# Double-width GpSimd products, e in place of d, fourth buffers and a new order in a fused recurrence and highway layer

## Chip, cores and metric

The kernel runs on one core of a Trainium2 chip. The metric is device time in microseconds (us) of one execution, the median of several runs. Engines are named as the profile has them: PE is TensorE, DVE is VectorE, ACT is ScalarE, POOL is GpSimd, SP is the engine that issues the DMAs.

## The reference

Four sequences of 6,336 tokens with 256 channels pass a gated recurrence and then a highway layer:

```python
sig = 1.0 / (1.0 + np.exp(-f_logit))
f = lower_bound + (1.0 - lower_bound) * sig
for t in range(S):
    h = f[:, t] * h + (1.0 - f[:, t]) * x[:, t]
    y[:, t] = h
...
H = np.maximum(y @ w_h, 0.0)
T = 1.0 / (1.0 + np.exp(-(y @ w_t + b_t)))
return T * H + (1.0 - T) * y
```

Inputs and output are float32. `lower_bound` and `b_t` have 256 entries, the weights are 256 x 256.

## The kernel before

The 25,344 tokens are cut into 28 units (L42 to L71): two of 256 tokens, one of 512, twenty-three of 1,024, one of 512, one of 256. Every unit passes the same operations, each a small function `do_<letter>`. The text `order` (L72 to L124) is a list of such operations, and it alone sets the program: `f12.1:2` calls `do_f` for unit 12, half 1, with buffer 2, a `v` behind it puts the operation on VectorE, and a number behind the colon is the buffer. Operations are kept in this order on each engine (`keep_in_program_order`); between engines only data and buffers hold them. All loads and writes stand in SP's one queue, so a write that waits for its copy holds up the loads behind it.

For one unit of 1,024 tokens, with channels in two halves of 128:

- l and x (L260): loads of 1 MB each, tokens on the partitions, in 6 buffers each.
- u (L274): ScalarE, sigmoid of -l, 3 buffers.
- bv (L282): u times x, in pairs of token blocks (512 columns an instruction, four instructions), on GpSimd or VectorE, 3 buffers.
- uT and bT (L288, L308): TensorE transposes u and bv so that channels lie on the partitions and tokens along the columns. f (L299, or L297 on VectorE) is made of uT.
- y (L325): VectorE's scan along the tokens, the recurrence, from f and bT. It carries its last value from unit to unit, and a unit that holds the start of a sequence has two scans for a half.
- z and g (L337 and L140): TensorE's products of y with the two weights, for each half. t (L350): ScalarE's sigmoid of z. d (L354): VectorE, from y and g, 3 buffers.
- e = d times t (L359), in a tile of its own, 3 buffers. The last field of a unit is a cut: columns below it go to GpSimd in pieces of 512 (`do_E`), the rest in one VectorE instruction (`do_e`).
- op (L378, L379): TensorE transposes back and adds, y through `diag` and e through the identity. o (L388): the copy to SBUF, mostly on ScalarE. Then the write (L393) of 512 KB.

`shared` (L203) makes a GpSimd product wait for the VectorE product (or weight preparation) that stands last ahead of it in the order text:

```python
def shared(ins, gpsimd):
    if not gpsimd:
        held[:] = [ins]
    elif held:
        tc.add_manual_dep(ins.ins, held.pop().ins.name, ...)
```

Ahead of the units stand the parameters (`cc`, `dg`, `WH`, `WT`) and idle matmuls that keep TensorE's clock up (`k*16`, L149 to L153).

## Time and profile before

| what | value |
|---|---|
| three executions | 211.55, 211.85 and 212.19 us, median 211.85 |
| profiled execution: span | 210.1 us (the page gives no other time of it; the median is 1.75 us more) |
| busy: PE, DVE, ACT, POOL | 192.2, 193.0, 194.5 and 174.0 us |
| DMA | 78.69 MB, on average 374 GB/s |
| instructions | 4,667 |

A group of instructions in the profile is shown as line, engine, operation, output <- inputs with shape and type, x its number | busy us, mean ns of one | the engine's idle time just before them and what ended it. In the timeline the columns are start, length, engine, line and operation, and in brackets the idle time before and what ended it. Neighbouring VectorE instructions overlap by some 0.09 us in their records and GpSimd's by some 0.05, so what one costs its engine is the distance of two starts.

### The profile page before, as it was taken

What the parts mean: (1) busy time and instruction counts of PE and PEld (TensorE: products, weight loads), DVE (VectorE), ACT (ScalarE), POOL (GpSimd) and SP (SyncE); (2) the same over time, 40 slices, a digit from 0 to 9 for tenths busy, and PEclk for the clock granted to TensorE, in tenths of its full rate; (3) what the DMA queues carried; (4) which work ended last, traced back from release to release, by engine and by line L of the source; (5) the groups of instructions that cost most, each with busy time, mean ns of one, the idle gap of its engine ahead of it and who ended that gap; (6) DMA issues with size and microseconds to landing.
All of it is one profiled execution on the core that took longest, in us unless ns stands there. A gap on an engine that the chain in (4) does not pass through costs nothing.

```text
span 210.1 us, 4667 instructions
## 1 busy us (share of the span) xinstructions
PE 192.2 (91%) x1819; PEld 132.4 (63%) x1819; DVE 193.0 (92%) x154; ACT 194.5 (93%) x190; POOL 174.0 (83%) x166
## 2 busy tenths in 40 slices
PE   7967798899989989999999999999999899999981
PEld 2444555576655766767576667657775676776760
DVE  0689999999999999999999999999999999999950
ACT  4678999999999999999999999999999999997882
POOL 3068989789999599978999999889879969999630
PEclk9999999999999999999999999999999999999998
DMA  6999999999999999999999999999999998463486
GB/s 223 392 426 421 410 418 424 420 415 420 410 428 413 420 420 403 331 406 387 387 427 416 409 416 423 418 417 396 333 428 416 416 413 332 188 271 132 172 328 254
DMA packets 15982, 78.69 MB, mean 374 GB/s; under 512 B 1748, under 2 KB 2264, under 8 KB 10072
## 3 DMA queue, kind: packets, MB, share of 16 engines
q1 hardware_dynamic: 15952, 78.39, 92.9%
q8 instruction: 14, 0.23, 0.5%
q14 instruction: 8, 0.07, 0.1%
q10 hardware_dynamic: 8, 0.00, 0.0%
HBM read 52.43 MB, written 25.95 MB: 373 GB/s over the span
## 4 chain that ended last, share of the span: by engine, by line
DVE 34%; PE 34%; DMA 12%; issue 8%; POOL 5%; ACT 3%; SPq 1%; POOLq 0%; DVEq 0%; ACTq 0%
DVE y L325 21%; DMA x<-in_x_dram 12%; DVE d L354 10%; PE op L379 5%; PE op L378 5%; PE g L337 4%; PE z L337 4%; PE bT L308 4%; POOL bv L282 4%; PE g L140 4%; PE uT L288 4%; PE z L140 3%; DVE e L359 3%; ACT t L350 2%; ACT o L388 1%
## 5 line engine op out<-in xcount | busy, mean ns | idle before, releaser
L282 POOL TENSOR_TENSOR bv<-u,x 128x512 bf16<-128x512 f16 x96 | 110.2, 1178 | 22.3 <-DVE w_sb L235 8.9
L325 DVE TENSOR_TENSOR_SCAN y<-f,y,bT 128x1024 bf16<-128x1024 f16 (+5 forms) x54 | 107.2, 1994 | 1.4 <-issue 0.4
L359 POOL TENSOR_TENSOR e<-d,t 128x512 bf16<-128x512 bf16 (+1 forms) x59 | 65.0, 1125 | 8.3 <-DVE e L359 5.0
L354 DVE SCALAR_TENSOR_TENSOR d<-y,ncc,g 128x1024 bf16<-128x1024 bf16 (+2 forms) x56 | 63.1, 1140 | 1.8 <-PE g L337 1.3
L350 ACT ACTIVATE t<-z,bt 128x1024 bf16<-128x1024 f32 (+2 forms) x56 | 58.4, 1066 | 2.7 <-PE z L140 1.5
L299 ACT ACTIVATE f<-uT,ncc 128x1024 f16<-128x1024 f16 (+2 forms) x54 | 57.8, 1079 | 2.0 <-ACT f L299 1.0
L388 ACT COPY o<-op 128x1024 f32<-128x1024 f32 (+1 forms) x50 | 52.3, 1058 | 1.9 <-PE op L379 1.0
L274 ACT ACTIVATE u<-l 128x2048 f16<-128x2048 f32 (+2 forms) x28 | 49.0, 1760 | 4.1 <-DMA l<-in_f_logit_dram 4.1
L378 PE MATMUL op<-diag,y 128*128 128x128 f16 x396 | 49.4, 219 | 0.8 <-ACT t L350 0.5
L379 PE MATMUL op<-ident_b,e 128*128 128x128 bf16 x396 | 49.4, 219 | 0.6 <-POOL e L359 0.6
L379 PEld LDWEIGHTS <-e 128*128 128x128 bf16 x396 | 44.0, 113 | 4.6 <-POOL e L359 1.1
L378 PEld LDWEIGHTS <-y 128*128 128x128 bf16 x396 | 44.2, 113 | 2.5
L337 PE MATMUL z<-y,w_sb 128*128 128x512 bf16 (+1 forms) x112 | 39.2, 367 | 2.0 <-DVE d L354 1.0
L337 PE MATMUL g<-y,w_sb 128*128 128x512 bf16 (+1 forms) x112 | 39.6, 367 | 0.5 <-DVE y L325 0.3
L308 PE MATMUL bT<-ident_f,bv 128*128 128x128 f32 x198 | 31.9, 278 | 4.1 <-DVE y L325 1.9
L288 PE MATMUL uT<-ident_h,u 128*128 128x128 f16 x396 | 31.1, 220 | 4.5 <-DVE y L325 3.3
L288 PEld LDWEIGHTS <-u 128*128 128x128 f16 x396 | 26.3, 98 | 13.9 <-issue 7.4
L140 PE MATMUL g<-y,w_sb 128*128 128x512 bf16 x92 | 34.9, 379 | 0.0
L140 PE MATMUL z<-y,w_sb 128*128 128x512 bf16 x92 | 34.8, 379 | 0.0
L337 PEld LDWEIGHTS <-w_sb 128*128 128x128 f16 x224 | 21.6, 98 | 16.2 <-issue 0.8
L308 PEld LDWEIGHTS bT<-ident_f,bv 128*128 128x128 f32 x198 | 22.3, 141 | 12.0 <-POOL bv L282 4.5
L140 PEld LDWEIGHTS <-w_sb 128*128 128x128 f16 x184 | 17.9, 98 | 18.2 <-issue 3.9
(35 smaller groups left out, 47.1 us busy)
## 6 DMA issues: line engine op xcount, KB each, us to landing
out_dram<-o SPq DMA_DIRECT2D x48, 512.0 KB, 6.1
l<-in_f_logit_dram SPq DMA_DIRECT2D x23, 1024.0 KB, 10.2
x<-in_x_dram SPq DMA_DIRECT2D x23, 1024.0 KB, 11.1
l<-in_f_logit_dram SPq DMA_DIRECT2D x2, 512.0 KB, 9.2
x<-in_x_dram SPq DMA_DIRECT2D x2, 512.0 KB, 6.0
l<-in_f_logit_dram SPq DMA_DIRECT2D x3, 256.0 KB, 6.1
x<-in_x_dram SPq DMA_DIRECT2D x3, 256.0 KB, 5.4
out_dram<-o SPq DMA_DIRECT2D x3, 256.0 KB, 5.4
```

The source lines that it names most:

```text
L140: return pe.add_instruction(mybir.InstMatmult(name=nc.get_next_instruction_name(), start_tensor_calc=start, stop_tensor_calc=stop, tile_si ...
L282: shared(pin(e.tensor_mul(st[n]["bv"][:, k].rearrange("p d j -> p j d"), st[n]["u"][:, q:q + 2], st[n]["x"][:, q:q + 2])), not eng)
L288: pin(nc.tensor.transpose(uT[:, j * P:(j + 1) * P], st[n]["u"][:, j, h * P:(h + 1) * P], ident_h))
L299: pin(nc.scalar.activation(to, of, AF.Identity, scale=ncc[:, h:h + 1], bias=1.0))
L308: pin(nc.tensor.transpose(words[:, k:k + g * (P - 1) + 1:g], pair, ident_f))
L325: pin(nc.vector.tensor_tensor_scan(y[:, c:e], st[n]["f", h][:, c:e], st[n]["bT", h][:, c:e], 0.0 if fresh else carry[h], op0=ALU.mult, op1 ...
L337: pin(nc.tensor.matmul(p[:, a:e], w, half(n, "y", ki)[:, a:e], start=ki == 0, stop=ki == NH - 1))
L350: pin(nc.scalar.activation(half(n, "t", m), st[n]["z", m][:, :tokens(n)], AF.Sigmoid, bias=bt[:, m:m + 1]))
L354: pin(nc.vector.scalar_tensor_tensor(half(n, "d", m), half(n, "y", m), ncc[:, m:m + 1], st[n]["g", m][:, :tokens(n)], op0=ALU.mult, op1=AL ...
L359: shared(pin(eng.tensor_mul(st[n]["e"][:, a:e], st[n]["d"][:, a:e], st[n]["t"][:, a:e])), eng is nc.gpsimd)
L378: pin(nc.tensor.matmul(o, half(n, "y", h)[:, cols], diag[:, h], start=True, stop=False))
L379: pin(nc.tensor.matmul(o, half(n, "e", h)[:, cols], ident_b, start=False, stop=True))
```

## The change

bv becomes instructions of 1,024 columns (two in a unit of 1,024 tokens). e is written over d, and d, u and bv have four buffers. e comes in fixed pieces (1,024, 512 and 512 columns in a unit of 1,024 tokens), and each piece can be on GpSimd or VectorE. The order text is new from the first operation to the last; with it l has four buffers (six before) and x five (six before). The lines below are cut to the core; of the order text only the first and last lines are shown.

```diff
-    units = [
-        (0, 128, 2, 0, 'y', 4, 512),
...
-        (0, 128, 8, 3072, 'y', 4, 1792),
-        (0, 128, 8, 4096, 'y', 4, 2048),
...
+    parts = [2] * 2 + [4] + [8] * 23 + [4] + [2]
+    units, at = [], 0
+    for nb in parts:
+        units.append((nb, at, {2: (0, 1), 4: (0, 1, 2), 8: (0, 2, 4)}[nb], {2: (0, 256, 512), 4: (0, 512, 1024), 8: (0, 1024, 1536, 2048)}[nb]))
+        at += nb * P
...
-pc:1 l0:0 u0:0 l3:1 wh cc dg i0.0:1 x0:0 i0.1:0 k*16 u3:1 wt WH b0.0v:0 l1:2 f0.0:0 f0.1:1 p0.1:0 i3.1:1 u1:2 s0.1:0
-WT p0.0:0 x1:1 s0.0 f3.1:2 l2:3 x2:2 i1.1:0 u2:0 g0.1:2 f1.1:3 i1.0:1 d0.1:0 g0.0:0 b1.0:1 x3:3 p1.0:0 f1.0v:1 s1.0:1
...
-E26.1 w24.1 d27.0 z27.0:2 c25.1:1 w25.0 t27.0 E26.0 o26.0:1 w25.1 c26.0:3 e27:0 E27.0 o27.0:2 c27.0:0 w26.0 w27.0
+l0:0 l1:1 u0:0 x0:0 u1:1 wh wt l3:2 x1:1 pc:0 l2:3 x2:2 cc i0.1:0 x3:3 b0.0v:0 f0.1:0 i1.1:1 f1.1:1 i0.0:0 p0.1:1 l4:0
+f0.0:2 p0.0:0 dg b1.0:0 WT x4:4 s0.0:0 WH s0.1 k*16 i1.0:0 f1.0v:0 u3:0 u2:2 g0.0:0 d0.0:0 l5:1 p1.0:1 p1.1:0 z0.1:1
...
+s27.0 e25.2 z27.1:2 d26.0:1 w23.1 d26.1 z26.0:0 z27.0:1 t27.1:1 w24.1 t26.0 o25.1:2 w25.0 t27.0 e26.1v e26.0v g27.0:0
+c25.1:1 d27.0:0 o26.0:1 g27.1:0 e27.0v w25.1 d27.1 c26.0:0 e27.1v o27.0:0 w26.0 c27.0v:2 w27.0
...
     def do_b(n, k, eng, slot):
         if "bv" not in st[n]:
             st[n]["bv"] = sb([P, NB // 2, D, 2], BF16, "bv", slot)
-        q = 2 * k
+        a, c = units[n][2][k:k + 2]
         e = nc.vector if eng else nc.gpsimd
-        shared(pin(e.tensor_mul(st[n]["bv"][:, k].rearrange("p d j -> p j d"), st[n]["u"][:, q:q + 2],
-                                st[n]["x"][:, q:q + 2])), not eng)
+        shared(pin(e.tensor_mul(st[n]["bv"][:, a:c].rearrange("p k d j -> p k j d"),
+                                st[n]["u"][:, 2 * a:2 * c].rearrange("p (k j) d -> p k j d", j=2),
+                                st[n]["x"][:, 2 * a:2 * c].rearrange("p (k j) d -> p k j d", j=2))), not eng)
...
-    def times(n, eng, a, e, slot):
-        flat(n, "e", "e", slot)
-        shared(pin(eng.tensor_mul(st[n]["e"][:, a:e], st[n]["d"][:, a:e], st[n]["t"][:, a:e])), eng is nc.gpsimd)
-
-    def do_E(n, k, eng, slot):
-        times(n, nc.gpsimd, k * 512, min(units[n][6], k * 512 + 512), slot)
-
     def do_e(n, k, eng, slot):
-        times(n, nc.vector, units[n][6], NH * tokens(n), slot)
+        a, c = units[n][3][k:k + 2]
+        e = nc.vector if eng else nc.gpsimd
+        shared(pin(e.tensor_mul(st[n]["d"][:, a:c], st[n]["d"][:, a:c], st[n]["t"][:, a:c])), not eng)
...
-                pin(nc.tensor.matmul(o, half(n, "e", h)[:, cols], ident_b, start=False, stop=True))
+                pin(nc.tensor.matmul(o, half(n, "d", h)[:, cols], ident_b, start=False, stop=True))
```

## Prediction

> **What bounds the kernel now.** I read the page's busy times first.

> ```profile
> PE 192.2 (91%) x1819; PEld 132.4 (63%) x1819; DVE 193.0 (92%) x154; ACT 194.5 (93%) x190; POOL 174.0 (83%) x166
> ```

> Three engines stand within 2.3 us of each other, so shares alone decide nothing. Next come VectorE's busy times by stretch (columns: start and end, length, busy time and number of instructions, granted clock, DMA share, GB/s).

> ```profile
> core 0: us, DVE busy (x), PEclk, DMA share, GB/s
> 0.00:16.00 16.00, 8.38 (x24) 1.00 0.91 348
> 16.00:34.00 18.00, 17.05 (x14) 1.00 1.01 417
> 34.00:160.00 126.00, 125.69 (x84) 1.00 1.01 407
> 160.00:200.00 40.00, 39.50 (x29) 1.00 0.71 285
> 200.00:210.10 10.10, 2.43 (x6) 0.91 0.74 288
> ```

> From 34 to 200 us VectorE is idle for 0.81 us in all. Its work is the span, but for 8.6 us lost ahead of 34 us and 7.7 us behind 200 us. GpSimd is the engine with idle time; where that lies is read from the groups and the timeline.

> ```profile
> L282 POOL TENSOR_TENSOR bv<-u,x 128x512 bf16<-128x512 f16 x96 | 110.2, 1178 | 22.3 <-DVE w_sb L235 8.9 <-DVE e L359 7.8 <-DVE bv L282 1.8
> L359 POOL TENSOR_TENSOR e<-d,t 128x512 bf16<-128x512 bf16 x54 | 61.8, 1167 | 3.8 <-DVE e L359 1.9 <-ACT o L388 1.8
> L359 POOL TENSOR_TENSOR e<-d,t 128x256 bf16<-128x256 bf16 x5 | 3.4, 670 | 4.5 <-DVE e L359 3.1 <-ACT t L350 1.5
> L359 DVE TENSOR_TENSOR e<-d,t 128x2048 bf16<-128x2048 bf16 x4 | 4.8, 1215 | 0.1
> L359 DVE TENSOR_TENSOR e<-d,t 128x1024 bf16<-128x1024 bf16 x1 | 0.7, 684 | 0.0
> ```
> ```profile
> 70.91 2.36 DVE L359 TENSOR_TENSOR e<-d,t 128x2048 bf16<-128x2048 bf16 x2
> ```
> ```profile
> 73.36 6.83 POOL L282 TENSOR_TENSOR bv<-u,x 128x512 bf16<-128x512 f16 x6 [2.41 <-DVE e L359]
> 174.53 0.67 POOL L359 TENSOR_TENSOR e<-d,t 128x256 bf16<-128x256 bf16 x1
> 175.16 1.17 POOL L282 TENSOR_TENSOR bv<-u,x 128x512 bf16<-128x512 f16 x1
> ```

> Two things are to be seen. GpSimd's idle time is mostly a wait for VectorE's own e products (7.8 + 5.0 us in ten waits, by the waits): the code makes it wait for each of them (L208), and it pays about VectorE's duration (2.41 us for a pair of 2.36). And six 512-wide products take 6.83 us, so one follows another every (6.83 - 1.18)/5 = 1.13 us. A 256-wide one is followed after 0.63 us (175.16 - 174.53). GpSimd is just in time, too: the last line is unit 24's last bv, ended at 176.3, and by the timeline VectorE starts that unit's first scan at 177.79.

> **Work moved.** Counted from the order strings:
> - bv on GpSimd: 96 of 512 columns become 6 of 512 and 44 of 1,024. e on GpSimd: 54 of 512 and 5 of 256 become 40 of 512, 2 of 256 and 15 of 1,024. GpSimd's e columns rise from 28,928 to 36,352.
> - VectorE: 16 e products (13.7 us) become 22. By its rows (280, 684 and 1,215 ns at 256, 1,024 and 2,048 columns) 512 takes about 0.42; 4 x 0.28 + 10 x 0.42 + 8 x 0.68 = 10.8 us. It gains one f of 1,024 (1.28) and one of 256 (0.48), two double-width bv in place of two single (2 x 0.54) and one output copy of 1,024 columns (twice 0.68, less a start: 1.2). With the 0.09 us by which neighbours overlap, the sum is +0.3 us.
> - ScalarE loses those f and that copy: 1.18 + 0.47 + 1.08 = 2.7 us. TensorE's matmuls are the same in number and size.

> **The open price: a 1,024-wide GpSimd product.** No row shows one. Upper end: twice a 512, 2.26 us (nothing in the rows falls with width). Lower end: 1.13 us, a 512's own. From 256 to 512 the interval grows by 0.50, so two more such steps give 1.13 + 1.00 = **2.13 us**, which I take, being the nearest rows' slope. A merged pair then saves 0.13 us. [...]

> **GpSimd's path.** The fourth unit's x load sets its start. Loads land in the order issued: 2.25 MB at 9.2 us (u1 waits for it), 5.5 MB at 17.47 (u4), so 2.55 us per MB. In the new order x4 ends at 6.5 MB: 17.47 + 2.55 = 20.0 us. From b4.0 to the end of unit 24's bv GpSimd then has 54 products of 1,024 (115.0 us at 2.13) and 34 of 512 (38.4), with ten VectorE products among them for which it makes way, 5.4 us by the e rows (five of 1,024 and four of 512 e, and one 1,024-wide bv). End: 20.0 + 115.0 + 38.4 + 5.4 = 178.8. The transposes and the wait to the scan add 0.6. VectorE from there has 27.0 us of work (scans 12.7, d 9.1, e 4.1, the rest 1.0), and 1.3 of small gaps as before in that stretch; then 0.7 from the last e through TensorE to the last copy, which is now VectorE's, and 3.6 for the last write (206.53 to 210.1 now). Sum: 178.8 + 0.6 + 28.3 + 4.3 = 212.0. GpSimd's other waits came to 3.4 us over that stretch before (its real end of unit 24 against the same sum); being fuller it should see less, so I add 1.2: **span 213.2 us**.

> **VectorE's path, for comparison.** Head: x5 has 8.5 MB ahead in place of 9.5, and the loads behind it start later, so its bv no longer waits (1.0 and 0.4 us for x5 and x6 now); TensorE's 16 warming matmuls come behind the first transposes of bv. Ahead of unit 5's first scan, at 34.06 us now, stand 25.5 us of VectorE's work and 8.6 idle; in the new order 25.3 us of work (e of unit 0 comes in, a copy goes out) and 6.1 idle, 4.7 until the parameters come (5.01, as now) and 1.4 around x1. GpSimd's path agrees: 20.0 + four bv at 2.13 + two e at 1.13 + 0.6 = 31.4. That is 2.6 us gained; I count 2.5. Tail: VectorE is idle 7.7 us after 200 us now, and would be 4.9 (0.7 + 3.6 and some 0.6 of waits): 2.7 gained. Sum: 210.1 - 2.5 - 2.7 + 0.3 = 205.2. GpSimd's path is 8 us longer, so GpSimd ends it: VectorE, near full now, gets waits for bT late in the kernel.

> **Costed at nothing.** e in place of d frees e's buffers, but a d buffer is now held until the output matmuls have read it; the d four or fewer units on may wait for TensorE. Now the longest such wait is 0.6 us and GpSimd's lateness covers it; uncovered, it is bounded by a few times 0.6. l has four buffers in place of six and x five in place of six: loads start later. A 1 MB load of l lands after 10.2 us (median), and DMA is only 0.71 busy from 160 us on, so there is slack; uncovered, ScalarE's wait for l (4.1 us in all now) would about double. More buffers alone, without an earlier producer, gain nothing.

> **Rivals.**
> 1. *Wide products are cheap, the change works (faster).* If the fixed part of a product is much larger than the 256 row says, GpSimd's path shrinks by 54 us per us. At 1.98 us it meets VectorE's 205.2, and VectorE ends it: span about 206, 208 measured. At 2.07 it meets today's 210.1: **2.07 us decides the sign**. For: GpSimd spans are rough and the 256 row has five members. Against: its slope. The same side is reached at 2.13 us if GpSimd never makes way for VectorE's products: 213.2 - 5.4 = 207.8.
> 2. *No fixed part at all.* At 2.26 us: 213.2 + 54 x 0.13 = 220.2, measured 222.
> 3. *VectorE's products meet a running GpSimd product.* GpSimd runs late against the order, so the wait in the code no longer keeps them apart. In a collision the VectorE product would stand until the GpSimd one ends: half of 2.13 us each, ten times, 205.2 + 10.7 = 215.9 by VectorE's path, 217.7 measured. These lines bear on it:

> ```profile
> 43.09 1.16 POOL L359 TENSOR_TENSOR e<-d,t 128x512 bf16<-128x512 bf16 x1
> ```
> ```profile
> 44.05 1.01 DVE L359 TENSOR_TENSOR e<-d,t 128x1536 bf16<-128x1536 bf16 x1
> ```

> The VectorE product began 0.20 us before GpSimd's end and took 1.01 us against 0.95 for its kind: a small stretch, no proof. [...]
> 4. *The orders cancel*: within 1 us of 210.1, if the price is near 2.07.

> **How the numbers follow.** The executions shown have a median of 211.85, the profiled span is 210.1; I add the same 1.75 us. Forecast 213.2 + 1.75 = **215.0 us**. Chances: forecast 0.40 and rival 3 0.08 (211.5 to 218.5 together), rival 1 0.34 (206.5 to 210.5), rival 2 0.11 (218.5 to 223), rival 4 0.07. The likeliest one's own range is 211.5 to 218.5. Cases of both signs hold most of the chance, so the range is 207.0 to 220.5. 0.3% is about what a measurement here can tell from no change: faster 0.36, same 0.06, slower 0.58.

> **What would show it.** The mean of the 1,024-wide rows (2.16 us expected, as 2.13 plus the overlap); GpSimd over 180 us busy, waits for inputs few; VectorE waiting for bT from unit 12 on, several us in all; ScalarE and TensorE idle beside it. A row of 2.0 us or less, or VectorE still gapless, proves me wrong; a DMA wait for l above 5 us would name another cause.

## The result, and the profile after

| | before | changed |
|---|---|---|
| median of the runs side by side | 211.74 us | 222.95 us (220.35 to 228.32) |
| ratio | | 1.0434 [1.0399, 1.0469] |
| profiled execution | span 210.1 us | 220.35 us, span 218.2 us |

The changed kernel is 4.3% slower; forecast were 215.0 us and at most 220.5. The ratio leaves out runs at a visibly lower clock; the spread belongs to the finding, so medians over all runs are given too. The page's busy times:

```profile
PE 190.3 (87%) x1794; PEld 132.1 (61%) x1819; DVE 205.5 (94%) x163; ACT 193.2 (89%) x187; POOL 183.0 (84%) x118
```

VectorE has 12.5 us more busy time, though the change gives it 0.3 us more of work by the count. Its busy times by stretch (length, busy and number, granted clock, DMA share, GB/s):

```profile
core 0: us, DVE busy (x), PEclk, DMA share, GB/s
0.00:16.00 16.00, 9.54 (x26) 1.00 0.89 346
16.00:34.00 18.00, 16.98 (x13) 0.91 1.02 419
34.00:160.00 126.00, 126.00 (x82) 1.00 0.99 386
160.00:200.00 40.00, 40.00 (x26) 1.00 0.80 313
200.00:218.20 18.20, 12.99 (x21) 0.98 0.61 241
```

It has no gap at all from 34 to 200 us, in which it ends 105 instructions (111 before; the table lists one that crosses a bound twice). So it doesn't wait for bT, which was forecast: it is slower inside its instructions. The groups by shape show where:

```profile
L256 POOL TENSOR_TENSOR bv<-u,x 128x1024 bf16<-128x1024 f16 x44 | 94.7, 2174 | 5.7 <-ACT u L248 1.9 <-DMA x<-in_x_dram 1.6 <-DVE bv L256 1.4
L335 POOL TENSOR_TENSOR d<-d,t 128x1024 bf16<-128x1024 bf16 x15 | 32.9, 2192 | 2.0 <-DVE d L335 1.9
...
L335 DVE TENSOR_TENSOR d<-d,t 128x1024 bf16<-128x1024 bf16 x8 | 14.3, 1783 | 0.0
L335 DVE TENSOR_TENSOR d<-d,t 128x512 bf16<-128x512 bf16 x10 | 6.7, 669 | 0.4 <-ACT t L325 0.2
```

GpSimd's wide products cost what was forecast. VectorE's e products of 1,024 columns took 1,783 ns on the mean; undisturbed they take 0.68 us (512: 0.41; 256: 0.28; a bv of 1,024: 1.30). Summed over its 25 products the excess is 13.1 us, and 0.1 us over the 19 of before. The worst one, in the timelines of the two engines:

```profile
165.79 4.34 DVE L335 TENSOR_TENSOR d<-d,t 128x1024 bf16<-128x1024 bf16 x1
```
```profile
165.24 4.34 POOL L335 TENSOR_TENSOR d<-d,t 128x512 bf16<-128x512 bf16 x3
169.83 2.31 POOL L256 TENSOR_TENSOR bv<-u,x 128x1024 bf16<-128x1024 f16 x1 [0.25 <-DMA x<-in_x_dram]
```

VectorE's product begins in the first of three GpSimd products (512, 1,024 and 512 columns; the row shows the form of the first) and ends 4.34 us later, at 170.13: just after GpSimd stopped for 0.25 us to wait for a load. It did not get in at the two ends of products in between. Ten other collisions ended at the end of the running product, or a little behind it, with an excess of 0.2 to 2.0 us each.

### The profile page after: what moved, and what is told of

Read it like the earlier page. It is cut to its first block, busy times and chain, and to the rows that moved or that the text cites. A ratio compares the mean times of both kernels' runs of the same rounds, so it can differ in the third digit from the quotient of the medians.

```text
span 218.2 us, 4593 instructions
## 1 busy us (share of the span) xinstructions
PE 190.3 (87%) x1794; PEld 132.1 (61%) x1819; DVE 205.5 (94%) x163; ACT 193.2 (89%) x187; POOL 183.0 (84%) x118
## 4 chain that ended last, share of the span: by engine, by line
PE 34%; DVE 29%; issue 13%; DMA 11%; POOL 5%; ACT 4%; SPq 2%; DVEq 0%; POOLq 0%; ACTq 0%
DVE y L300 17%; DMA x<-in_x_dram 11%; DVE d L329 6%; PE op L349 5%; PE op L348 5%; PE bT L283 5%; PE z L312 5%; PE g L312 4%; DVE d L335 4%; PE uT L263 3%; PE g L114 3%; PE z L114 3%; POOL d L335 3%; ACT u L248 3%; POOL bv L256 2%
## 5 line engine op out<-in xcount | busy, mean ns | idle before, releaser
L256 POOL TENSOR_TENSOR bv<-u,x 128x1024 bf16<-128x1024 f16 (+1 forms) x50 | 101.6, 2053 | 15.4 <-DMA x<-in_x_dram 11.0
L335 POOL TENSOR_TENSOR d<-d,t 128x512 bf16<-128x512 bf16 (+2 forms) x57 | 81.5, 1450 | 8.3 <-DVE d L335 4.4
L325 ACT ACTIVATE t<-z,bt 128x1024 bf16<-128x1024 f32 (+2 forms) x56 | 56.7, 1033 | 7.4 <-PE z L114 6.1
L274 ACT ACTIVATE f<-uT,ncc 128x1024 f16<-128x1024 f16 (+2 forms) x52 | 53.9, 1048 | 3.3 <-PE uT L263 1.7
L358 ACT COPY o<-op 128x1024 f32<-128x1024 f32 (+1 forms) x49 | 48.3, 1010 | 4.2 <-PE op L349 3.2
L349 PE MATMUL op<-ident_b,d 128*128 128x128 bf16 x396 | 49.2, 219 | 1.0 <-DVE d L335 1.0
L349 PEld LDWEIGHTS <-d 128*128 128x128 bf16 x396 | 44.1, 113 | 5.3 <-issue 1.9
L283 PE MATMUL bT<-ident_f,bv 128*128 128x128 f32 x198 | 32.2, 280 | 10.2 <-DVE y L300 6.1
L283 PEld LDWEIGHTS bT<-ident_f,bv 128*128 128x128 f32 x198 | 22.2, 141 | 20.3 <-DVE y L300 8.1
L263 PEld LDWEIGHTS <-u 128*128 128x128 f16 x396 | 26.6, 99 | 10.2 <-issue 2.9
L114 PE MATMUL g<-y,w_sb 128*128 128x512 bf16 x83 | 31.4, 379 | 0.1
L114 PE MATMUL z<-y,w_sb 128*128 128x512 bf16 x81 | 30.7, 379 | 0.1
```

The lines of the kernel that those rows point to most:

```text
L114: return pe.add_instruction(mybir.InstMatmult(name=nc.get_next_instruction_name(), start_tensor_calc=start, stop_tensor_calc=stop, tile_si ...
L256: shared(pin(e.tensor_mul(st[n]["bv"][:, a:c].rearrange("p k d j -> p k j d"), st[n]["u"][:, 2 * a:2 * c].rearrange("p (k j) d -> p k j d" ...
L263: pin(nc.tensor.transpose(uT[:, j * P:(j + 1) * P], st[n]["u"][:, j, h * P:(h + 1) * P], ident_h))
L283: pin(nc.tensor.transpose(words[:, k:k + g * (P - 1) + 1:g], pair, ident_f))
L325: pin(nc.scalar.activation(half(n, "t", m), st[n]["z", m][:, :tokens(n)], AF.Sigmoid, bias=bt[:, m:m + 1]))
L335: shared(pin(e.tensor_mul(st[n]["d"][:, a:c], st[n]["d"][:, a:c], st[n]["t"][:, a:c])), not eng)
```

## Experiments

"Excess" is always the time of VectorE's operations on SBUF beyond their undisturbed durations. Two theories ran through the first rounds: *collisions* (VectorE's products lose time beside GpSimd's) and *GpSimd's path* (the forecast). The collision theory was later split: A, a product can stand through several GpSimd products; B, it waits for the running one only. A2, a later form of A: it stands where a long row of GpSimd products without a pause lies before it.

### One input in place of two

```diff
+        if eng:
+            half_of = st[n]["d"][:, a:c].rearrange("p (k j) -> p k j", j=2)[:, :, 0]
+            shared(pin(nc.vector.tensor_scalar(half_of, half_of, 0.5, None, op0=ALU.mult)), False)
+            return
```

> The changed kernel, but every e product on VectorE is replaced by a one-input multiplication of every second column of d by 0.5, which takes about as long (so those pieces of e are wrong: t is left out). Collision theory (a VectorE product with two SBUF inputs stands still while a GpSimd product runs; this added 13 us to VectorE's path of 205): VectorE's extra time goes, VectorE busy falls from 205.5 to about 193, span 205 to 207, time 207 to 209. GpSimd-path theory (my forecast: GpSimd's load ends the kernel): 207.8 to 213 span, 209.5 to 215 measured, with waits of the scan for bT of several us. Theory that the new order or the fewer l and x buffers cost the time: stays at 219 to 221.

Measured: 223.05 us, ratio 1.0421 [1.0361, 1.048]; profiled span 225.2. By the time alone, the theory of order and buffers comes nearest. But the trace shows why nothing was gained: the substitute collides too, with an excess of 17 us. One scale of 0.30 us took 8.00 us beside five GpSimd products. So it is not the second input that matters. This was a bad control, but the 8.00 us showed that a wait may be longer than one product.

### Wide products split in place

```diff
-        shared(pin(e.tensor_mul(st[n]["d"][:, a:c], st[n]["d"][:, a:c], st[n]["t"][:, a:c])), not eng)
+        step = c - a if eng else min(c - a, 512)
+        for a in range(a, c, step):
+            b = a + step
+            shared(pin(e.tensor_mul(st[n]["d"][:, a:b], st[n]["d"][:, a:b], st[n]["t"][:, a:b])), not eng)
```

(bv likewise.)

> The changed kernel with each 1,024-wide GpSimd product issued as two of 512 in the same place. Collision theory: what is left of a running product is half as long, so VectorE's extra time falls from 13 us to 5 to 8 and VectorE's path to 210 to 213; GpSimd's own work grows by 59 times 0.13 = 7.7 us, so it may be the later one: span 212 to 217, measured 214 to 219. GpSimd-path theory: the longer GpSimd work alone counts, 8 us more than the changed kernel: 226 to 229 measured. Theory that the order and the buffers cost the time: unchanged, 220 to 222.

Measured: 243.23 us (238.06 to 243.63); profiled span 241.5. Both theories missed by far. The trace has an excess of 32.2 us, and 27.7 of it lies in three products, which stood through eight further GpSimd products each:

```profile
182.30 10.10 DVE L341 TENSOR_TENSOR d<-d,t 128x1024 bf16<-128x1024 bf16 x1
```

### The kernel before with e in place and fourth buffers

```diff
-        shared(pin(eng.tensor_mul(st[n]["e"][:, a:e], st[n]["d"][:, a:e], st[n]["t"][:, a:e])), eng is nc.gpsimd)
+        shared(pin(eng.tensor_mul(st[n]["d"][:, a:e], st[n]["d"][:, a:e], st[n]["t"][:, a:e])), eng is nc.gpsimd)
```

> The kernel before in its own order, with e written over d and four buffers of d, u and bv used in turn. Collision theory: nothing of this touches the meeting of VectorE and GpSimd products, within 0.3% of 211.7. Theory that holding d until the output matmuls costs VectorE waits: 213 to 216.

Measured: 211.39 us, ratio 0.9986 [0.9976, 0.9995]. These parts of the change cost nothing.

### The kernel before with wide products alone

```diff
-z3.0:1 E2.1 b5.3:2 f5.0:2 t3.0:0 i5.1:1 p4.1:0 g3.0:2 b5.1 o2.0:0 b5.0 z3.1:1 s4.1 f5.1:3 b5.2 d3.0 w0.0 p5.0:1 w1.0
+B5.1:2 f5.0:2 t3.0:0 i5.1:1 p4.1:0 g3.0:2 B5.0 o2.0:0 z3.1:1 s4.1 f5.1:3 d3.0 w0.0 p5.0:1 w1.0 B6.1:0 u7:2 i7.1:0
...
```

(`B` is a pair of `b` joined to 1,024 columns; 44 pairs of bv and 21 of e are joined, each at the place of its first.)

> The kernel before in its own order, with neighbouring GpSimd pieces of one unit joined to 1,024 columns at the place of the first (44 pairs of bv, 21 of e). GpSimd's work falls by 65 times 0.13 = 8 us. Collision theory: the order was laid out for 512-wide products, VectorE's e now begin while a GpSimd product runs; 11 of them in the middle, 0.5 to 1.1 us each: VectorE's path 5 to 12 us longer, 216 to 223 measured. GpSimd-path theory: less GpSimd work can only help, 209 to 212.

Measured: 215.07 us, ratio 1.0161 [1.0146, 1.0176], span 213.2: between the two expectations, 1 us below the collision theory's. GpSimd's busy time falls from 174.0 to 165.5 us, and the kernel is 3.1 us longer. The excess of VectorE's products is 3.4 us, in five of them that met a wide one. The width, with the second of each pair moved up to the first, is enough to make the old order collide. It accounts for 3 of the change's 8 us of span; the new order is the main other difference.

### The changed kernel without the wait of `shared`

```diff
-            held[:] = [ins]
+            held[:] = []
```

> The changed kernel without the wait that makes GpSimd's next product in the order wait for the VectorE product before it. Theory A: that wait is one of the few things that stop GpSimd; without it a VectorE product stands longer, the extra time of VectorE's products rises from 13.1 to 20 us or more and the span to 224 to 260 us. Theory B: a product waits only for the running one, so the extra time stays at 10 to 14 us, GpSimd loses its waits, and the span is 215 to 219 us.

Measured: 233.19 us (221.1 to 235.56); profiled span 229.2 with an excess of 21.7 us. One product of 0.41 us took 6.68 us. That is theory A's; one of the four runs took 221.1 us, which theory B would allow as well, so it is the trace that decides here, not the time.

### VectorE's nine e products of the middle left out

```diff
-d6.0 e6.1 e6.0 w3.1 f9.0:0 l11:0 o4.0:2 e6.2v c4.0:0 x10:0 b10.0:2 o4.1:0 p8.0:0 e5.0v c4.1:1 w4.0 i10.0:1 f10.0:1
+d6.0 e6.1 e6.0 w3.1 f9.0:0 l11:0 o4.0:2  c4.0:0 x10:0 b10.0:2 o4.1:0 p8.0:0  c4.1:1 w4.0 i10.0:1 f10.0:1
...
```

> The changed kernel without VectorE's nine products of units 5 to 20 (these columns of d go out without the factor t). Collisions as the cause (A and B): VectorE loses 5.0 us of its own and about 12 of the 13.1 us that it stood, so its path falls from 218.2 to 201 us and GpSimd's ends the kernel, 208 by the recorded sum less the 5.4 us of VectorE products in it: span 201 to 208, measured 203 to 210 us. If the time went elsewhere (the new order, the clock of TensorE), only the 5.0 us go: span 213, measured 215 us.

Measured: 226.13 us, ratio 1.0694 [1.0663, 1.0724], span 223.4: less work, and slower than the changed kernel. Expected were 203 to 215. The trace says why; the one VectorE product left in the middle, bv of unit 19, stood through seven GpSimd products:

```profile
131.36 12.55 DVE L255 TENSOR_TENSOR bv<-u,x 128x1024 bf16<-128x1024 f16 x1
```

### And that product given to GpSimd

```diff
-b19.1v
+b19.1
```

> As the run that left out VectorE's nine products of units 5 to 20 (these columns go out without the factor t), and the one VectorE product that was left there, bv of unit 19, is given to GpSimd, so that from 17 to 190 us VectorE has no operation on SBUF alone. Theory A: that one product stood 12.6 us in the run before; without it VectorE's path is 201 us and GpSimd's, 208 by the recorded sum less 5.4, with 2.1 us more of bv, sets the end: span 203 to 211, measured 205 to 213 us, and its runs agree within 1%. If the time of the changed kernel goes elsewhere (order, TensorE's clock): span 218 to 224 again.

Measured: 220.28 us, ratio 1.0407 [1.0389, 1.0425], span 217.1; the four runs lie within 1 us. Nothing stands any more (excess 2.2 us, nearly all at the two ends), and VectorE's busy time is 190.7 us. But the span is 217.1 and not 203 to 211, so here the collision theory's figure missed: TensorE now waits for GpSimd's bv. The waits of TensorE ahead of the transposes of bv:

```profile
PE bT L282 <- POOL bv L255: 9.2, 7, 5.3
PE bT L282 <- DVE y L299: 1.8, 4, 0.7
```

In the changed kernel it was the other way round (6.1 us for VectorE's y in the same list, 2.9 for bv). More than half of the 9.2 us is one wait, and this edit made it: in the order, the given product (`b19.1`) stands behind both bv of unit 20, so on GpSimd it comes third in a row of three.

```profile
138.39 6.33 POOL L255 TENSOR_TENSOR bv<-u,x 128x1024 bf16<-128x1024 f16 x3
```
```profile
144.78 0.69 PE L282 MATMUL bT<-ident_f,bv 128*128 128x128 f32 x2 [5.26 <-POOL bv L255]
```

VectorE is idle for 5.76 us with it. GpSimd starts unit 4 at 21.6 us here (20.3 in the changed kernel), has 2.1 us of bv more, and ends unit 24's bv at 182.1. The recorded sum, less its 5.4 us of VectorE products and with the 2.1 us of bv and the 1.2 us that the forecast allowed for other waits, gives 178.8 - 5.4 + 2.1 + 1.2 = 176.7. The 5.4 us that are missing are GpSimd's own waits, 6.6 us in place of 1.2 (a later start and slightly cheaper products, about 1.5 us each, cancel). Of the 6.6 us, 4.9 lie behind the hole at 139 to 145 us, so what GpSimd's path would be without it is not shown.

### Another form of the product

```diff
+        if eng and 4 < n < 21:
+            shared(pin(nc.vector.scalar_tensor_tensor(st[n]["d"][:, a:c], st[n]["d"][:, a:c], 1.0, st[n]["t"][:, a:c],
+                                                      op0=ALU.mult, op1=ALU.mult)), False)
+            return
```

> The changed kernel with VectorE's nine products of units 5 to 20 written as scalar_tensor_tensor (d times 1.0 times t), as d is computed but with both operands in SBUF. By the durations of d it should take 1.26 for 0.68 us (1,024 columns) and 0.74 for 0.41 (512): 4.2 us more in all. If this form is not held by GpSimd: 205.2 + 4.2 = span 209, measured 209 to 213 us. If it is held like the product: span 218 to 224, measured 219 to 226 us.

Measured: 232.9 us (220.1 to 234.6); three of the four runs lie above the 226 us expected. It is held too: the profiled run, at 217.9, has these products at up to 3.15 us for 1,024 columns, which d takes in 1.26.

### Products by themselves, each GpSimd product waiting for the one before

```python
    i = pin(nc.gpsimd.tensor_mul(a[:, :w], a[:, :w], b[:, :w]))
...
    i = pin(nc.vector.tensor_mul(c[:, :512], c[:, :512], d[:, :512]))
```

(a is overwritten in place, so each GpSimd product waits for the one before.)

> This kernel computes no output of the reference; it times products by themselves. GpSimd multiplies 1,024 columns five times (or 512 columns eight times) with no wait between, and VectorE does work from PSUM of 0.3 to 2.5 us and then one operation on SBUF alone. Theory A (a VectorE operation whose operands are all in SBUF begins only when GpSimd stops between two products, and a queue of products without a wait gives it no stop): the 512-column product, 0.41 us by itself, takes up to 8 to 10 us, to the end of the fifth (eighth) GpSimd product, in some or all of the sixteen places. Theory B (it waits for the running product to end, no longer): 0.4 to 2.5 us beside 1,024 columns and 0.4 to 1.5 us beside 512, the rest of the running product plus 0.41. Of the other forms (scalar_tensor_tensor of two SBUF operands, one-input scale and copy, a product with one operand in PSUM, in fp32, mixed): by the traces so far the PSUM one keeps its time, the one-input scale is held like the product; for the other forms no trace has a row, each is either held (over 1.5 us) or keeps its time (under 0.9 us).

Measured: in all sixteen places the product got in at the next end of a GpSimd product (0.42 to 2.25 us): theory B. Of the forms, only one kept its time, the one with an operand in PSUM (300.63); the product (61.00) and the one-input scale (255.72) are shown, and scalar_tensor_tensor, copy, fp32 and mixed products took 1.8 to 2.4 us in place of 0.29 to 0.69:

```profile
61.00 2.17 DVE L118 TENSOR_TENSOR c<-c,d 128x512 bf16<-128x512 bf16 x1
...
255.72 2.04 DVE L122 TENSOR_SCALAR h<-c 128x512 bf16<-128x512 bf16 x1
...
300.63 0.68 DVE L126 TENSOR_TENSOR p<-c,g 128x512 bf16<-128x512 bf16 x1
```

### The same, GpSimd's products free of each other

```diff
-    i = pin(nc.gpsimd.tensor_mul(a[:, :w], a[:, :w], b[:, :w]))
+    i = pin(nc.gpsimd.tensor_mul(r[k][:, :w], a[:, :w], b[:, :w]))
```

> This kernel computes no output of the reference. As the measurement of the products by themselves, but no GpSimd product waits for the one before it (there each did, and 0.07 us lay between two): six of 1,024 or eight of 512 columns in a row, VectorE's 512-column product arriving 0.2 to 2.1 us after the first began, each arrival twice; and six rows of 512 in which each GpSimd product waits for a ScalarE operation done long before. Theory A in its new form (a VectorE operation on SBUF gets in only where GpSimd is idle between two products, and a product that waits for nothing begins without that pause): the product of 0.42 us stands to the end of the row, up to 12.6 us (1,024) and 8.8 us (512), in most or some of the arrivals. Theory B (it gets in at the next end of a product in any case): at most 2.6 us beside 1,024 and 1.6 us beside 512 columns, everywhere, as where each waited.

Measured: 0.42 to 2.30 us in all 54 places. Theory A in this form fell: being free of waits is not enough.

### Each GpSimd product waits for the one before, in the changed kernel

```diff
+        if gpsimd:
+            if prev:
+                tc.add_manual_dep(ins.ins, prev.pop().ins.name, ...)
+            prev[:] = [ins]
```

> The changed kernel, all its work, with one thing added: each GpSimd product waits for the one before it, which leaves about 0.08 us between two. Theory A in its new form: no VectorE product stands longer than the running product and itself (2.6 us), the extra time of VectorE's products falls from 13.1 to 8 to 11 us, the runs no longer differ by 8 us but by under 2, and the span is 213 to 217, unless GpSimd's path, longer by 88 times 0.06 to 0.1 us, ends it at up to 220. Theory B: nothing changes but GpSimd's longer path: 218 to 222 us.

Measured: 223.84 us (222.8 to 224.06), ratio 1.0567 [1.0547, 1.0588]. No product stood longer than 2.95 us, the excess was 10.4 us, and the runs agree within 1.3 us; but GpSimd's lengthened path (unit 24's bv ends at 187.1, 180.7 in the changed kernel) takes it all back, more than expected: the span, 221.6, is where the other theory had it, and only the trace and the agreement of the runs speak for this one. The micro-rows and this run together left one difference to look at. In the traces of the kernels, a product had stood only where nine or more GpSimd products had run without a pause ahead of it; the rows by themselves had been eight long.

### Long rows by themselves

GpSimd has 40 products of 512 columns (or 24 of 1,024), VectorE one product m d-like operations later:

```python
    for m in (2, 6, 8, 10, 12, 14, 16, 20, 24, 28, 32):
        row(512, 40, m)
```

> This kernel computes no output of the reference. GpSimd multiplies 40 times 512 (or 24 times 1,024) columns with no wait between; VectorE works from PSUM for 2.4 to 40 us and then has one 512-column product (or the scalar_tensor_tensor, or the one-input scale) on SBUF. Theory A2 (what lets the product wait past the running GpSimd product is a row of nine or more without a pause before it): arrivals within the first five products wait 0.4 to 2.5 us, those after nine or more stand in most cases to the end of the row, 10 to 35 us; with each GpSimd product waiting for the one before, never more than 1.6 us. Theory B (the row doesn't matter; in the kernel other engines' work does it): at most 1.6 us beside 512 and 2.6 us beside 1,024, everywhere.

Measured: this is it. Up to the twelfth product of the row the VectorE product got in at the next end (0.47 to 1.36 us). From the 14th on it stood to the end of the row: 29.12, 26.49, 23.85, 18.60, 13.35, 8.07 and 2.82 us. At 1,024 columns it got in in the 14th and stood in the 18th (13.56 us). The first that stood, with GpSimd's row:

```profile
237.93 29.12 DVE L86 TENSOR_TENSOR c<-c,d 128x512 bf16<-128x512 bf16 x1
```
```profile
222.42 44.35 POOL L102 TENSOR_TENSOR r<-a,b 128x512 bf16<-128x512 bf16 x40 [0.34 <-DVE c L86]
```

222.42 + 44.35 = 266.77, and the product ends at 267.05: its own 0.4 us came behind the whole row. The two scalar_tensor_tensor and the two one-input scales stood alike (18.86 and 18.48 us in the 24th). With each product waiting for the one before, arrivals in the 22nd and 30th got in (1.18 and 0.47 us). And in a row in which VectorE had a product every 5.7 us, none stood.

### Where the limit lies, and what counts as a pause

```python
    for m in (9, 10, 11, 12, 13):
        for more in ((), (256,)):
            row(512, 30, m, more)
...
    for m in (14, 16, 20, 28):
        row(512, 40, m, (), 12)
```

> This kernel computes no output of the reference. Rows of GpSimd products as before, VectorE's 512-column product arriving at a finer step. If a count of products without a pause decides: it gets in up to the 12th product and stands to the end of the row from the 13th to 15th on, alike for 512 and 1,024 columns. If a time decides: from 13 to 16 us of row, so for 1,024 columns from the 7th or 8th product on, which the last rows speak against. Rows in which each (or every second) product waits for a ScalarE operation long done: if such a wait is a pause, the product never stands; if not, it stands in all eight, 9 to 25 us. Rows with one pause ahead of the 13th product: if it starts the count again, arrivals in the 16th to 23rd product get in and that in the 32nd stands; if not, all four stand, 8 to 26 us.

Measured: at 512 columns one arrival in the 14th product got in and another, 0.8 us later in it, stood; all later ones stood. At 1,024 columns arrivals up to the 14th got in, and of five in the 15th to 17th three stood. So a count decides, with a limit of some 14 to 17 products, not a time: 13 products take 14 us in one row and 27 in the other. GpSimd products that wait for something long done are no pause: all eight stood (8.06 to 23.84 us). One pause starts the count again: behind it, arrivals 4, 6 and 11 products on got in, and one 20 on stood (8.25 us). The two arrivals in the same product:

```profile
226.94 1.15 DVE L87 TENSOR_TENSOR c<-c,d 128x512 bf16<-128x512 bf16 x1
...
261.57 18.09 DVE L87 TENSOR_TENSOR c<-c,d 128x512 bf16<-128x512 bf16 x1
```

The kernels' traces fit, if the count starts at a pause or at VectorE's last operation on SBUF (the row in which VectorE came every 5.7 us says that this restarts it too). In thirteen traces of the kernels 70 VectorE operations met a GpSimd product with another ready behind it. 53 had fewer than nine products counted ahead of them: all got in. Five had nine: one stood. Twelve had 13 to 26: ten stood, and the two that got in are both of the scalar_tensor_tensor run.

### A pause after every fourth GpSimd product, in the changed kernel

```diff
+        if gpsimd:
+            if len(prev) == 4:
+                tc.add_manual_dep(ins.ins, prev[-1].ins.name, ...)
+                prev.clear()
+            prev.append(ins)
```

> The changed kernel, all its work; every fourth GpSimd product waits for the one before it, a pause of about 0.08 us for some 27 products, 2 to 3 us of GpSimd's time in all. Theory A2: no VectorE product stands through more than the rest of a group of four; the runs agree within 2 us, and the span is that of GpSimd's path, 214 to 218 us (measured 216 to 220). Theory B: stands and spread as in the changed kernel, 220 to 228 us measured.

Measured: 220.75 us (218.88 to 221.62), ratio 1.0417 [1.0384, 1.045]; the changed kernel beside it 227.67 us. Nothing stood longer than 2.62 us; excess 10.8 us. So the long stands are gone, as theory A2 has it, though the runs still differ by 2.7 us (under 2 expected). The gain is 7 us by the medians, but by the ratios, 1.0417 against 1.0502, only some 1.8 us. It shows how little is left to gain: still 4% slower than before.

### The changed kernel again

> The changed kernel itself again. If standing VectorE products make the spread: the fastest runs 220 to 221 us, others at 222 to 229; in a trace of a run over 224 us VectorE's products take 5 us or more beyond the 13.1 us of the first trace. If TensorE's clock makes it, they take 13 us there too, and the clock alone is lower.

Measured: 227.67 us (220.95 to 232.69), ratio 1.0502 [1.0452, 1.0552]. The new trace (223.68 us, span 221.5) has an excess of 14.9 us, and in it a product that took 2.17 us in the first trace:

```profile
55.51 8.69 DVE L335 TENSOR_TENSOR d<-d,t 128x512 bf16<-128x512 bf16 x2
```
```profile
50.55 8.48 POOL L256 TENSOR_TENSOR bv<-u,x 128x1024 bf16<-128x1024 f16 x4
58.98 4.34 POOL L335 TENSOR_TENSOR d<-d,t 128x512 bf16<-128x512 bf16 x3
63.68 2.52 POOL L256 TENSOR_TENSOR bv<-u,x 128x1024 bf16<-128x1024 f16 x1 [0.36 <-DVE d L335]
```

Of the 8.69 us for two products, 8.09 are the first, which stood until GpSimd came to the product that waits for it by `shared`. The same program, at the same place, got in once and stood once: some of the spread is made here. The difference is a load. In the second trace GpSimd had run 16 products without a pause when VectorE came; in the first it had stopped for x two products earlier, and the count was two:

```profile
50.67 8.66 POOL L256 TENSOR_TENSOR bv<-u,x 128x1024 bf16<-128x1024 f16 x4 [0.44 <-DMA x<-in_x_dram]
```

The second span is 3.3 us longer, with 1.8 us more excess: a stand can cost more than its length. TensorE's work in that stretch shows one way (length, busy and number, granted clock, DMA share, GB/s):

```profile
56.00:60.00 4.00, 3.19 (x20) 1.00 1.02 414
60.00:64.00 4.00, 0.00 (x0) 0.96 1.01 403
64.00:68.00 4.00, 1.44 (x6) 0.50 0.49 207
68.00:72.00 4.00, 4.00 (x39) 0.68 0.00 0
72.00:76.00 4.00, 4.00 (x61) 1.00 0.80 274
```

TensorE stands still with VectorE for four microseconds and then has half its clock for about four more (0.50, then 0.68 on the mean of the next four). The first trace has it on a smaller scale: behind 1.04 us of idle time up to 19.07 us the clock is 0.50 from 20 to 22 us. In the kernel before, the idle matmuls of the head fill TensorE from 5.31 to 9.69 us, and the clock there is 1.00. The trace falls short of the 224 us from which 5 us of further excess were expected, and the runs over 227 us were not traced, so whether all of the spread comes from there stays open.

### The kernel before without the wait of `shared`

(The same edit.)

> The kernel before without the wait that makes GpSimd's next product in the order wait for VectorE's product before it. In the kernel before VectorE's 19 products took 0.1 us more than undisturbed. Theory A2: they now meet running rows of GpSimd products; 13 of them in the middle wait for half of 1.13 us each, 7 us, and some stand longer: span 214 to 235. Theory B: 13 times 0.57 us, less what GpSimd gains: span 210 to 217. If GpSimd is never there when VectorE comes: 209 to 210.

Measured: 222.79 us (218.2 to 222.89). The excess goes from 0.1 to 10.3 us, one product of 0.95 us taking 5.12. So what the kernel before pays for in GpSimd's waits (7.8 + 5.0 us in the prediction's groups) buys back 6.5 us (the shortest run) to 11 us (the median): its VectorE products begin where GpSimd has just been stopped.

### The end of the kernel before

```diff
-        (0, 128, 4, 24576, 'y', 4, 768),
-        (0, 128, 2, 25088, 'y', 4, 256),
+        (0, 128, 4, 24576, 'y', 4, 0),
+        (0, 128, 2, 25088, 'y', 4, 0),
...
-E26.1 w24.1 d27.0 z27.0:2 c25.1:1 w25.0 t27.0 E26.0 o26.0:1 w25.1 c26.0:3 e27:0 E27.0 o27.0:2 c27.0:0 w26.0 w27.0
+d27.1:0 g27.0:2 z27.1:1 t27.1:0 w24.1 d27.0 z27.0:2 c25.1:1 w25.0 t27.0 e27:0 o26.0:1 w25.1 c26.0:3 o27.0:2 c27.0v:0
```

> The kernel before with one thing changed at its end: the e products of the last two units, of 512 and 256 tokens, all on VectorE (half of unit 26 and a part of unit 27 were GpSimd's), and the last copy on VectorE. GpSimd's last products took 1.1 and 0.6 us where VectorE's take 0.3 to 0.7, in a stretch where VectorE idles: 1.5 to 2.5 us less, 209.2 to 210.3 us measured. If the tail hangs on the last tokens' chain through TensorE and the store alone: 211.3 to 212 us, as before.

Measured: 211.91 us, ratio 1.0012 [1.0003, 1.0021]. Not a gain. No version here beats the kernel before by more than 0.3%.

## Why the prediction was wrong

- **A wide GpSimd product at 2.13 us: right.** Two that follow each other take 4.26 us in the timeline with 2.15 for one: 2.11 us. Rival 2 is out. GpSimd's price goes nearly with the columns here: a product of 256 is followed after 0.63 us, one of 512 after 1.13, one of 1,024 after 2.11, and 2,048 columns by themselves took 4,045 ns in the run of products by themselves.
- **GpSimd's path: near, as far as it is shown.** Unit 24's last bv ends at 180.7 us (forecast 178.8). With the forecast's terms behind it (0.6 + 28.3 + 4.3) that is 213.9, an estimate; 213.2 was forecast. So in the first trace the span, 218.2, is only some 4 us above what GpSimd's path would give. By this estimate that, and not the whole 13.1 us of excess, is about what the collisions are worth there; GpSimd's own waits for them may add a little. The run with VectorE's products out of the way doesn't settle it: its 217.1 us have 2.1 of bv that isn't GpSimd's in the change, 1.2 of a later start, and a hole that the edit itself made. The forecast's 5.4 us of VectorE products are not in that run; GpSimd's own waits, put at 1.2 us and 6.6 there, stand in their place.
- **VectorE's path at 205.2 us: the step that failed**, and with it "GpSimd's path is 8 us longer, so GpSimd ends it". Its head and tail were near (idle 17.1 to 12.7 us, 4.4 gained, 5.2 forecast), its work too; but its products were priced as if GpSimd were not there. With the 13.1 us of the first trace it is 218.3, and the span was 218.2. That it comes so close is luck: VectorE's other work was 0.9 us less than counted (205.5 - 13.1 = 192.4 for 193.3), and the head and tail gained 0.8 us less. But the span follows the excess in the traces of the changed kernel and of its variants with as many VectorE products: 217.2 us at 10.8 (a pause after every fourth), 218.2 at 13.1, 221.5 at 14.9, 225.2 at 17 (one input), 229.2 at 21.7 (without `shared`), 241.5 at 32.2 (split). Off this line lie the run with every product waiting (221.6 at 10.4), where GpSimd's path is longer, and the other form, whose products are longer by themselves. VectorE stayed gapless, which the prediction itself named as what would prove it wrong.
- **Rival 3 was the case, and its size was too small.** It had ten waits of half a product, 10.7 us, 217.7 measured, at a chance of 0.08. That a product stands until the running one ends was the author's assumption, which no line of before shows; the sixteen places of the products by themselves do (0.42 to 2.25 us). Eleven collisions cost 13.1 us in the first traced run, ten cost 14.9 in the second. What it lacked is the stand through a whole row, 4.1 to 12.6 us at once in these kernels, and with that the spread up to 228 and 232 us, beyond the range (whether all of the spread comes from stands is open).
- **Why its chance was too low.** The prediction saw that GpSimd would run late against the order, so that the wait in `shared` no longer keeps the two apart, and then judged by one line of before, where a product lost 0.06 us. But before is the kernel in which that wait still works: its trace could not show the price. Taking the wait out shows it at once, 10.3 us.
- **Rival 1** (faster below 2.07 us) is out by its price, 2.11.
- **e in place and fourth buffers at nothing: right** (0.9986).

Which VectorE operations meet GpSimd's is shown by the products by themselves: the one with an operand in PSUM kept its time (0.68 us beside GpSimd, and 0.68 on the mean of all four), the one-input scale took 2.04. And the long rows show that VectorE can wait much longer than one instruction, 29.12 us.

## What to carry to other kernels

A VectorE operation whose operands are all in SBUF is priced by what GpSimd does at that moment (here 0.42 us of work took from 0.42 to 29.12); where the two are lined up by a wait, count that wait as cover and ask who comes late once the order changes. Give GpSimd a real pause (a wait that is not yet met) at least every eight products (every fourth was tried, and nothing stood longer than 2.62 us; eight is by the counts above, 53 of 53 with fewer than nine got in), or keep VectorE's SBUF operations just behind a stop of GpSimd (0.1 us of excess over 19 products in the kernel before): a long free row held VectorE to its end. If a kernel's runs differ by several per cent, look in the traces for one instruction of many times its length. And before a collision is removed, estimate the path that ends next: here that left some 4 us to gain, by an estimate.
